# A planner that orders a kernel's instructions gets other numbers for its transfers: first landing later, 400 in place of 360

## The chip, the cores and the metric

The kernel runs on one core of a Trainium2 chip. The metric is device time in microseconds (us) of one execution, the median of several. Five engines take part: PE (TensorE, matrix products), DVE (VectorE), ACT (ScalarE), POOL (GpSimd) and SP (SyncE, which here only issues transfers). Each engine takes its instructions in the order in which they were emitted, and waits where an operand is not there yet.

## The reference, cut to what matters

```python
# x: (8, 8, 512, 64), state: (8, 8, 32, 64); weights are float64
a = softmax(scale * x @ state.T)         # per batch and head
xread = a @ state
a2 = softmax(scale * state @ x.T)
sread = a2 @ x
x = concat([xread, sread], tokens)       # 8 * 544 = 4352 tokens of 512
h = x @ w_in                             # 512 -> 1024
solu = h * softmax(h)
ln = layernorm(solu) * g_ln
y = ln @ w_out                           # 1024 -> 512
g = maximum(y @ w2_in, 0) ** 2           # 512 -> 2048
out = g @ w2_out                         # 2048 -> 512
```

## The kernel before, in words

Phase 1 goes batch by batch (b = 0 to 7). Per batch the kernel loads x in two layouts (xT and xn) and the block-diagonal states (bdf), makes the two score matrices (lines 358 to 470: products on PE, exponentials a_sb and eT on ACT at L433 and L400, sums, reciprocals and the scaling at L443 on DVE and POOL), builds the products sw of the state and the first layer's weights, and runs the first layer (hps, L635), the SoLU and the layer norm (L593 to L624), the transposes of its result (lnTp, L687; split in lt at L693 on ACT and L696 on DVE) and the second layer (y, L722). Most products are made in three passes over operands that are split in a high and a low part (a cast at L262 on ACT gives the high one, a subtraction at L268 on DVE or POOL the low one). Where PE turns to a piece that is not there, it waits.

The weights come as float64 and are decoded on the chip (`decode`, L284 to L327): a transfer of 512 KB into a buffer `raw` (three of them; `raw_u` at the start), an activation on ACT at L312 that reads it into `wi`, `dec` or `w`, a shift at L315 and a combination at L318 on DVE, and for most of them the cast and the subtraction. w_in and w_out are decoded at the start, into wi and wo. Later in phase 1 the weights of the third and fourth layers are decoded beside the other work, four pieces of 512 KB at a time, in six stretches, whose first loads are issued at about 108, 157, 206, 250, 295 and 339 us (the rest of the fourth layer's from 387 us on). They are summed as Strassen's method wants them, split in `w2s` and stored in DRAM as `w_d`.

Phase 2, from about 421 us on, makes the last two layers by Strassen's method, seven products instead of eight (h at L1144 and L1289 are its products on PE). It reads y back from DRAM (`yraw`), makes its sums (`load_y`, L891 to L941: yt, casts on ACT and subtractions and sums on DVE), and reads the weights from `w_d` into `w`.

The order of PE's work is written out by hand, in the order in which the program calls. The order of the other engines is not. All their work is given as tasks to a planner, the class `Flow` (line 31 on). It keeps one clock per engine in `free`, for DVE (V), ACT (A), POOL (P) and the transfers (D), and steps its own time `now` forward with PE's written order. `poll` goes through the tasks by how soon their results are due and emits the next instruction of a task once the task's operands are planned to be there and the engine planned to be free. `run` gives the planned end, which is the operand's time for the task's next step. So the planned time of a transfer decides which instructions stand in front of the one that reads what it brings, in each engine's queue. The kernel is planned twice, and the second plan uses the due times that the first one found. A transfer goes through `dma`, and its cost is its size over a rate:

```python
def run(self, eng, cost, ready, emit):
    start = max(self.free[eng], ready, self.now)
    self.free[eng] = start + cost
    emit(eng)
    return start + cost + (2.0 if eng == "D" else self.HOP)
...
def dma(out, in_, kb):
    return fl.run("D", kb / 360.0, 0.0, lambda e: nc.sync.dma_start(out=out, in_=in_))
```

All transfers are issued from SP in the order in which the planner emits them. Names: `wi`, `wo`, `dec`, `w` decoded weights; `w2s` and `w_d` split weights and their place in DRAM; `sps`, `hps`, `sTp`, `aTp`, `lnTp`, `ep`, `xsp`, `y`, `h` tiles in PSUM that PE writes; `ys` a copy of y that is stored; `u`, `e` the SoLU's tiles.

Of the kernel before, what the change touches and what calls it, by code (L numbers as in the profile page):

```python
# [31 lines left out]
class Flow:  # L32
# [12 lines left out]

    SPARE = {"V": 0.7, "A": 0.0, "P": 0.0, "D": 0.0}
    NEVER = 1e9

    def __init__(self, plan=None):

        self.plan, self.made = plan, []
        self.now = 0.0
        self.end = 0.0
        self.warm = self.WARM_UP
        self.free = {"V": 0.0, "A": 0.0, "P": 0.0, "D": 0.0}
        self.tasks = []
        self.later = []

# [9 lines left out]
    def spawn(self, gen, slack=8.0):  # L68


        task = {"gen": gen, "req": None, "done": None, "slack": slack, "costs": [],
                "by": self.NEVER, "n": len(self.made)}
        self.made.append(task)
# [36 lines left out]
    def latest(self, task):  # L110

        if self.plan:
            by, costs = self.plan[task["n"]]
            if by < self.NEVER:
                return by - sum(costs[len(task["costs"]):])
# [49 lines left out]
def attn_solu_relu2_kernel(  # L165
# [14 lines left out]
    nc = tc.nc  # L180
# [6 lines left out]
    B, P, T, _ = x_n.shape  # L187
    S = x_t.shape[3]
    HP = x_t.shape[2]
    H, D = 2 * HP, P // 2  # L190
# [13 lines left out]
    fl = Flow(plan)  # L204
# [36 lines left out]
    room = {"raw": 3, "dec": 3, "e": 2, "raw2": 3, "dec2": 2, "u": 8, "g": 3}  # L241

    def dma(out, in_, kb):
        return fl.run("D", kb / 360.0, 0.0, lambda e: nc.sync.dma_start(out=out, in_=in_))

    def take(name):
        def ok():
# [36 lines left out]
    def decode(dst_h, dst_l, src, pool=None, w=None, spare=False):  # L284
# [15 lines left out]
        if len(src.shape) == 3:  # L300
            tf = tf.rearrange("p (k f) -> p k f", k=src.shape[1])
        f = dma(tf, src, 512)
        own = w is None
        if own:
# [37 lines left out]
    def load_x(b):  # L342
        bdf[b] = ap_.tile([P, G, 192], F32, tag="bdf", name="bdf", bufs=2)
        done["st", b] = dma(bdf[b], bd[b], 192)
        xT[b] = ap_.tile([P, HP, S], F32, tag="xT", name="xT")
        done["xT", b] = dma(xT[b], x_t[b], 1024)
# [544 lines left out]
    def load_y(j):  # L891
        t0, n = groups[j]
        q = n * P
        for _, name, _ in PRODUCTS:
            done["y", j, name] = {"by": fl.NEVER, "done": None}

# [484 lines left out]
```

## Time and profile before

| | |
|---|---|
| median of 3 runs | 1096.95 us (1093.66 to 1098.14) |
| the profiled execution's own time | 1096.98 us |
| its span in the profile | 1095.1 us |
| mean granted clock of PE | 0.991 |
| PE busy | 1065.5 us, 97% of the span |
| DVE, ACT, POOL busy | 786.7, 589.4, 144.2 us |

The span lies 1.9 us below the execution's own time. PE is busy nearly throughout; the about 30 us in which it is not lie mostly ahead of 60 us. A row of the timeline gives the start in us from the span's start, the duration, the engine and line, the operation with output and input, and in brackets the idle time ahead of it on its engine with what ended it.

### The profile page before, as it was taken

How to read it: one execution, taken by the hardware profiler on the slowest of the kernel's cores; microseconds unless marked ns; L12 is line 12 of the kernel's file. 1: busy time of each engine (PE TensorE's matmuls, PEld its weight loads, DVE VectorE, ACT ScalarE, POOL GpSimd, SP SyncE). 2: the span in 40 equal slices, each digit the busy share in tenths (PEclk: the TensorE clock that was granted, in tenths of full speed). 3: DMA queues.
4: the chain of work that ended last, by engine and by line, in shares of the span. 5: the costliest groups of instructions: out<-in, count | busy, mean ns of one | idle time of the engine just before them, and what ended most of it. 6: DMA issues, size and time to landing. Idle time of an engine off the chain costs nothing.

```text
span 1095.1 us, 19407 instructions
## 1 busy us (share of the span) xinstructions
PE 1065.5 (97%) x7184; PEld 941.0 (86%) x7184; DVE 786.7 (72%) x1243; ACT 589.4 (54%) x992; POOL 144.2 (13%) x229
## 2 busy tenths in 40 slices
PE   4999998999999999999999999999999999999998
PEld 1467777777777888889998889999999999999998
DVE  6856776888887867868984479755688467855773
ACT  4948677787787765435453344533345334533442
POOL 1623332333434320000000000000000000000000
PEclk8989999999999999999999999999999999999999
DMA  9420553747526378998787777778889888898885
GB/s 352 169 85 24 177 211 124 278 146 244 212 87 241 138 259 272 309 320 260 193 249 229 195 201 204 231 233 265 253 270 304 282 252 277 264 312 254 249 262 159
DMA packets 126509, 247.70 MB, mean 226 GB/s; under 512 B 13520, under 2 KB 36048, under 8 KB 124368
## 3 DMA queue, kind: packets, MB, share of 16 engines
q1 hardware_dynamic: 126416, 246.47, 69.5%
q8 instruction: 57, 0.93, 0.4%
q14 instruction: 36, 0.29, 0.1%
HBM read 199.23 MB, written 47.19 MB: 225 GB/s over the span
## 4 chain that ended last, share of the span: by engine, by line
PE 89%; ACT 4%; DVE 3%; DMA 2%; issue 1%; POOL 1%; SPq 0%; ACTq 0%; DVEq 0%; POOLq 0%
PE h L1289 31%; PE h L1144 30%; PE y L722 15%; PE hps L635 7%; PE lnTp L687 2%; PE hps L376 1%; DMA raw_u<-w_in 1%; ACT u L624 1%; PE aTp L470 1%; DMA raw<-w_in 1%; ACT e L603 1%; PE srd L486 1%; PE sTp L414 0%; DMA raw<-w_out 0%; PE sps L376 0%
## 5 line engine op out<-in xcount | busy, mean ns | idle before, releaser
L1289 PE MATMUL h<-w,g 128*128 128x256 f32 x2856 | 343.5, 283 | 0.0
L1289 PEld LDWEIGHTS h<-w,g 128*128 128x128 f32 x2856 | 343.3, 192 | 0.2
L1144 PE MATMUL h<-yt,w 128*128 128x384 f32 (+1 forms) x1680 | 328.2, 356 | 0.5 <-ACT ys L262 0.5
L1144 PEld LDWEIGHTS h<-yt,w 128*128 128x128 f32 x1680 | 300.6, 188 | 27.0 <-ACT ys L262 0.7
L722 PE MATMUL y<-lt,wo 128*128 128x512 f32 (+1 forms) x864 | 219.2, 396 | 2.1 <-DVE sw L268 1.7
L262 ACT CAST g<-r 128x768 fp32r<-128x768 f32 (+1 forms) x140 | 128.3, 920 | 150.9 <-PE h L1289 147.6
L268 DVE TENSOR_TENSOR g<-r,g 128x768 fp32r<-128x768 f32 (+1 forms) x140 | 148.4, 1063 | 51.8 <-ACT g L262 51.2
L722 PEld LDWEIGHTS y<-lt,wo 128*128 128x128 f32 x864 | 150.3, 191 | 37.9 <-issue 6.7
L1108 DVE TENSOR_TENSOR r<-u,h 128x384 f32<-128x384 f32 (+1 forms) x120 | 72.1, 604 | 109.5 <-PE h L1144 109.1
L1094 ACT COPY u<-h 128x512 f32<-128x512 f32 (+2 forms) x160 | 81.3, 522 | 112.0 <-PE h L1144 85.4
L1190 DVE TENSOR_TENSOR r<-r 128x768 f32<-128x768 f32 (+1 forms) x100 | 104.9, 1060 | 21.1 <-ACT r L1180 20.8
L635 PE MATMUL hps<-sw,aT 128*128 128x512 f32 x368 | 98.3, 417 | 0.0
L635 PEld LDWEIGHTS hps<-sw,aT 128*128 128x128 f32 x368 | 69.8, 192 | 23.5 <-issue 6.2
L696 DVE SCALAR_TENSOR_TENSOR lt<-lnTp,g_sb,lt 128x512 fp32r<-128x512 f32 (+1 forms) x72 | 51.6, 716 | 25.6 <-ACT lt L693 24.8
L1182 DVE SCALAR_TENSOR_TENSOR r<-r 128x768 f32<-128x768 f32 (+3 forms) x80 | 65.2, 834 | 1.2
L1094 ACT ACTIVATE r<-h 128x384 f32<-128x384 f32 (+1 forms) x40 | 21.2, 531 | 82.3 <-PE h L1144 81.9
L693 ACT ACTIVATE lt<-lnTp,g_sb 128x512 fp32r<-128x512 f32 (+1 forms) x72 | 47.7, 662 | 31.4 <-PE lnTp L687 31.3
L268 POOL TENSOR_TENSOR w2s<-dec,w2s 128x512 fp32r<-128x512 f32 (+1 forms) x38 | 47.9, 1273 | 70.3 <-ACT w2s L262 50.3
L598 DVE SCALAR_TENSOR_TENSOR u<-u,e 128x1024 f32<-128x1024 f32 x34 | 42.5, 1249 | 5.9 <-ACT e L593 5.5
L268 DVE TENSOR_TENSOR yt<-yraw,yt 128x384 fp32r<-128x384 f32 (+1 forms) x70 | 41.3, 606 | 6.3 <-ACT yt L262 6.1
L687 PE MATMUL lnTp<-ident,u 128*128 128x128 f32 x272 | 42.6, 275 | 1.1 <-ACT u L624 1.1
L624 ACT ACTIVATE u<-u,nmu,vs 128x1024 f32<-128x1024 f32 x34 | 42.1, 1241 | 2.5 <-POOL nmu L619 2.5
(98 smaller groups left out, 909.6 us busy)
## 6 DMA issues: line engine op xcount, KB each, us to landing
w<-w_d SPq DMA_DIRECT2D x560, 256.0 KB, 3.4
w_d<-w2s SPq DMA_DIRECT2D x36, 512.0 KB, 3.2
raw<-w_out SPq DMA_DIRECT2D x24, 512.0 KB, 6.7
xT<-x_t SPq DMA_DIRECT2D x8, 1024.0 KB, 7.0
xn<-x_n SPq DMA_DIRECT2D x8, 1024.0 KB, 6.1
y_d<-ys SPq DMA_DIRECT2D x16, 512.0 KB, 3.7
raw<-w_in SPq DMA_DIRECT2D x16, 512.0 KB, 7.9
out<-u SPq DMA_DIRECT2D x28, 256.0 KB, 2.8
```

The source lines that it names most:

```text
L262: nc.scalar.copy(out=out, in_=in_)
L268: return lambda e: eng_of[e].tensor_tensor(out=out, in0=in0, in1=in1, op=ALU.subtract)
L624: f = yield {"A": 1.16}, f, lambda e: nc.scalar.activation(out=u, in_=u, func=AF.Identity, bias=nmu, scale=c)
L635: nc.tensor.matmul(out=ps, lhsT=lhsT(i, k), rhs=rhs(j, k)[:, cs], start=(k == 0 and n == 0), stop=(k == n_k - 1 and n == len(passes) - 1),)
L687: nc.tensor.transpose(ps[:, t, :], u_t[key, t][:, k * P:(k + 1) * P], ident)
L722: nc.tensor.matmul(out=ps, lhsT=wo[k][:, w, c * P:(c + 1) * P], rhs=o[:, a], start=(k == 0 and i == 0), stop=(k == K1 - 1 and i == 2),)
L1094: nc.scalar.activation(out=o, in_=src, func=func) if func else nc.scalar.copy(out=o, in_=src)
L1108: f = yield {"V": 0.15 + cols / 960}, max(at, box["task"]["done"]), lambda e: nc.vector.tensor_tensor(out=o, in0=box["t"], in1=src, op=ALU.add
L1144: nc.tensor.matmul(out=ps, lhsT=wt[:, e2, k], rhs=yy[:, e1, k], start=(p in ("P1", "P2", "P5") and k == 0 and s == 0), stop=(k == 1 and s ...
L1182: f = yield {"V": 0.15 + (2 - key[-1]) * q / 960}, f, lambda e: nc.vector.scalar_tensor_tensor(out=v, in0=v, scalar=0.0, in1=v, op0=ALU.ma ...
L1190: return lambda e: eng_of[e].tensor_tensor(out=out, in0=in0, in1=in1, op=op)
L1289: nc.tensor.matmul(out=where[i // 2][0][:, i % 2 * Q:i % 2 * Q + Q], lhsT=g[:, e1, m % 2, i * P:i * P + P], rhs=wt[:, e2], start=(p in ("P ...
```

## The change

The transfers' clock starts at 2.6 us instead of 0, and a transfer costs its KB over 400 instead of over 360. So a transfer of 512 KB is planned at 1.28 us instead of 1.42, and the first transfers land 2.6 us later in the plan, less what the rate gives back.

```diff
     SPARE = {"V": 0.7, "A": 0.0, "P": 0.0, "D": 0.0}
     NEVER = 1e9
+    FIRST_DMA = 2.6
...
-        self.free = {"V": 0.0, "A": 0.0, "P": 0.0, "D": 0.0}
+        self.free = {"V": 0.0, "A": 0.0, "P": 0.0, "D": self.FIRST_DMA}
...
     def dma(out, in_, kb):
-        return fl.run("D", kb / 360.0, 0.0, lambda e: nc.sync.dma_start(out=out, in_=in_))
+        return fl.run("D", kb / 400.0, 0.0, lambda e: nc.sync.dma_start(out=out, in_=in_))
```

No instruction is given other work. The order of PE's 6,722 instructions stays as it was; on DVE, ACT, POOL and SP instructions change places, and ten subtractions of the low parts go from POOL to DVE. All lines of the changed kernel lie one further down. Three places follow. (In these rows a count as x3 stands for instructions of the same kind in a row, and the numbers behind a name are those of its buffers.)

ACT at the start, from the decode of the fifth piece of w_in on (wi), with the two exponentials of the first softmax (a_sb), the copies sw and aT and the first pieces of w_out (dec); before:

```order
L312 ACTIVATE wi_126<-raw_u 128x512
L312 ACTIVATE wi_127<-raw_u 128x512
L433 ACTIVATE a_sb<-a_sb 128x512
L312 ACTIVATE wi_128<-raw_u 128x512
L262 COPY sw<-hps 128x512
L312 ACTIVATE wi_129<-raw_u 128x512
L262 COPY sw<-hps 128x512
L433 ACTIVATE a_sb<-a_sb 128x512
L262 COPY aT<-aTp 128x512
L312 ACTIVATE dec<-raw 128x512 x3
```

and now:

```order
L313 ACTIVATE wi_126<-raw_u 128x512
L313 ACTIVATE wi_127<-raw_u 128x512
L313 ACTIVATE wi_128<-raw_u 128x512
L434 ACTIVATE a_sb<-a_sb 128x512
L313 ACTIVATE wi_129<-raw_u 128x512
L263 COPY sw<-hps 128x512 x2
L313 ACTIVATE dec<-raw 128x512
L434 ACTIVATE a_sb<-a_sb 128x512
L263 COPY aT<-aTp 128x512
L313 ACTIVATE dec<-raw 128x512 x3
```

The first exponential has moved behind the seventh piece of w_in, the second one behind the first piece of w_out. Some rows on, four decodes instead of three stand ahead of the first SoLU's exponential (L593).

ACT in the second stretch with such decodes (about 155 to 177 us), from the copy xs on; dec are pieces of the third layer's weights, L693 the high part of lt, L593, L603 and L624 the SoLU and the layer norm; before:

```order
L262 COPY xs<-xsp 128x4x32
L693 ACTIVATE lt<-lnTp,g_sb 128x512
L593 ACTIVATE e,es<-u,hm 128x1024
L262 CAST w2s<-dec 128x2x256
L603 ACTIVATE e,vs<-u,us 128x1024
L312 ACTIVATE dec<-raw 128x512
L400 ACTIVATE eT,l_1705<-s_sb,m_1718 128x512
L433 ACTIVATE a_sb<-a_sb 128x512
```

and now:

```order
L263 COPY xs<-xsp 128x4x32
L263 CAST w2s<-dec 128x2x256
L694 ACTIVATE lt<-lnTp,g_sb 128x512
L594 ACTIVATE e,es<-u,hm 128x1024
L313 ACTIVATE dec<-raw 128x512
L604 ACTIVATE e,vs<-u,us 128x1024
L401 ACTIVATE eT,l_1712<-s_sb,m_1725 128x512
L434 ACTIVATE a_sb<-a_sb 128x512
```

The cast w2s has moved ahead of lt, and a first decode ahead of the SoLU's L603. Up to the last L603 and L693 of this stretch ACT now has four decodes where it had three. In the next three of these stretches (from 206, 250 and 295 us on) a decode likewise now stands ahead of the first L603, and four instead of three come within the stretch; the fourth came some 13 us or more later before.

ACT at the end of phase 1 (about 418 to 425 us), with the last copies of y (ys), the casts yt of the first products' operands and the decodes and casts of the fourth layer's weights (w); before:

```order
L262 CAST yt<-yraw 128x512
L262 COPY ys<-y_4438 128x256
L262 COPY ys<-y_4439 128x256
L262 CAST yt<-yraw 128x512
L262 COPY ys<-y_4440 128x256
L262 COPY ys<-y_4441 128x256
L312 ACTIVATE w_4282<-raw 128x512
L1094 COPY u_4642<-h_4629 128x512
```

and now:

```order
L263 COPY ys<-y_4443 128x256
L263 COPY ys<-y_4444 128x256
L263 COPY ys<-y_4445 128x256
L263 CAST yt<-yraw 128x512
L263 COPY ys<-y_4446 128x256
L263 CAST yt<-yraw 128x512
L263 CAST w_4283<-w_4283 128x256
L263 CAST w_4282<-w_4282 128x2x256
```

The casts yt have moved two places back, one of them in between the last two copies of y, and casts of weights stand where the first copies of h were. On SP a load of w_out, which needs a free raw buffer, has moved ahead of the twelve loads of `w` that were issued from 387.60 us on.

## Rows read from the trace of the kernel before

**Rows 1.** The page: busy time by engine.

```profile
PE 1065.5 (97%) x7184; PEld 941.0 (86%) x7184; DVE 786.7 (72%) x1243; ACT 589.4 (54%) x992; POOL 144.2 (13%) x229
```

**Rows 2.** Busy time by stretches; the last three columns: granted clock, DMA share, GB/s.

```profile
0.00:27.40 27.40, 11.06 (x64) 3.83 (x64) 16.67 (x35) 11.82 (x19) 3.03 (x8) 0.88 0.94 352
27.40:54.80 27.40, 24.70 (x188) 11.05 (x172) 24.39 (x49) 24.86 (x47) 17.14 (x25) 0.93 0.45 169
150.00:180.00 30.00, 26.71 (x210) 20.75 (x195) 19.94 (x43) 19.30 (x36) 7.64 (x15) 0.96 0.72 252
180.00:330.00 150.00, 150.00 (x1039) 115.73 (x1038) 127.75 (x247) 117.31 (x207) 56.45 (x91) 1.00 0.51 179
500.00:1095.10 595.10, 591.28 (x4181) 577.99 (x4179) 403.54 (x521) 249.61 (x395) 0.00 (x0) 1.00 0.80 245
```

**Rows 3.** PE's waits: for whom, us in total, times, longest.

```profile
PE aTp L470 <- POOL a_sb L443: 7.6, 2, 4.1
PE sTp L414 <- DVE lt L696: 3.3, 1, 3.3
PE h L1144 <- ACT ys L262: 0.5, 1, 0.5
```

**Rows 4.** Timeline of ACT, from the sixth piece of w_in to the first SoLU.

```profile
14.83 0.67 ACT L312 ACTIVATE wi<-raw_u 128x512 f32<-128x512 f32 x1 [0.61 <-DMA raw_u<-w_in]
16.11 0.67 ACT L312 ACTIVATE wi<-raw_u 128x512 f32<-128x512 f32 x1 [0.61 <-DMA raw_u<-w_in]
17.24 0.63 ACT L433 ACTIVATE a_sb<-a_sb 128x512 f32<-128x512 f32 x1 [0.46 <-DVE a_sb L268]
17.77 0.66 ACT L312 ACTIVATE wi<-raw_u 128x512 f32<-128x512 f32 x1
...
21.68 0.63 ACT L433 ACTIVATE a_sb<-a_sb 128x512 f32<-128x512 f32 x1 [1.74 <-DVE a_sb L268]
...
23.72 0.67 ACT L312 ACTIVATE dec<-raw 128x512 f32<-128x512 f32 x1 [0.38 <-DMA raw<-w_out]
```

**Rows 5.** Timeline of PE, around the second layer's start.

```profile
59.15 1.65 PE L722 MATMUL y<-lt,wo 128*128 128x512 f32 x3 [1.13 <-DVE sw L268]
```

**Rows 6.** Timeline of ACT in the second stretch with decodes.

```profile
174.38 0.66 ACT L312 ACTIVATE dec<-raw 128x512 f32<-128x512 f32 x1 [3.02 <-DMA raw<-w_in]
174.95 1.13 ACT L603 ACTIVATE e<-u,us 128x1024 f32<-128x1024 f32 x1
...
176.08 0.67 ACT L693 ACTIVATE lt<-lnTp,g_sb 128x512 fp32r<-128x512 f32 x1
```

**Rows 7.** Timeline of PE in the second stretch with decodes.

```profile
168.42 2.92 PE L635 MATMUL hps<-sw,aT 128*128 128x512 f32 x12
...
177.59 0.93 PE L414 MATMUL sTp<-ident,s_sb 128*128 128x128 f32 x4 [3.29 <-DVE lt L696]
179.59 3.71 PE L635 MATMUL hps<-sw,aT 128*128 128x512 f32 x12
```

**Rows 8.** Timeline of ACT in the third stretch with decodes.

```profile
219.79 1.15 ACT L603 ACTIVATE e<-u,us 128x1024 f32<-128x1024 f32 x1 [0.17 <-DVE u L598]
...
223.47 0.68 ACT L312 ACTIVATE dec<-raw 128x512 f32<-128x512 f32 x1 [1.69 <-DMA raw<-w_in]
```

**Rows 9.** Timeline of DVE in the third stretch with decodes.

```profile
221.96 0.75 DVE L696 SCALAR_TENSOR_TENSOR lt<-lnTp,g_sb,lt 128x512 fp32r<-128x512 f32 x1
```

**Rows 10.** Timeline of PE in the third stretch with decodes.

```profile
223.41 0.60 PE L414 MATMUL sTp<-ident,s_sb 128*128 128x128 f32 x4
```

**Rows 11.** Timeline of SP, at the end of phase 1: loads of w and of y.

```profile
387.60 9.67 SPq L244 DMA_DIRECT2D w<-w_d  x12
...
408.85 5.04 SPq L244 DMA_DIRECT2D yraw<-y_d  x2
```

**Rows 12.** Timeline of ACT, around the start of phase 2.

```profile
420.11 0.62 ACT L262 CAST yt<-yraw 128x512 fp32r<-128x512 f32 x1
420.63 0.65 ACT L262 COPY ys<-y 128x256 f32<-128x256 f32 x2
```

## The prediction

> **What bounds the kernel now.** I read the page first: PE is busy 97% of the span [rows 1]. The order of PE's instructions does not change, and neither does any instruction's work, so the time can only move where PE waits, or begins to wait, and where its clock falls behind a wait. The table by stretches says where that is [rows 2]: of the 29.6 us in which PE is not busy, 16.3 lie in the first 27.4 us and 2.7 in the next 27.4; 3.3 lie at 150 to 180 us; there is nothing at 180 to 330 us, and 3.8 after 500 us, where no wait on another engine is listed, so that is start and tail of a dense stretch. The list of PE's waits names the causes [rows 3]: the scaled softmax a_sb of the first batch (7.6 us in two waits), one wait of 3.3 us in the second stretch with decodes, and the copy ys at the start of phase 2 (0.5); about 60 us there is one of 1.13 for sw [rows 5]. Behind that PE is dense but for these, so what is lost or gained at the start is carried to the end.
>
> Next I asked which of the planner's numbers is right, since that is what the change is about. At the start ACT waits for each piece of w_in, and the decodes begin at 14.83 and 16.11 us, each at the end of such a wait [rows 4]: 1.28 us for 512 KB, which is 400 KB per us, not 360. So the new rate is the truer one for that stretch. That says the plan comes nearer to the transfers, not that the kernel gets shorter: an engine that takes its work in order loses wherever the plan puts a decode ahead of work that PE waits for and the piece lands later than planned.
>
> The Trainium skill speaks against the change here: its page "DMA: Bandwidth & Descriptors", section "Specifications", gives a limit of about 358 GB/s for the memory of one core, by which a piece of 512 KB (524 kB) takes 1.46 us and the old rate would have been the right one. The measured 1.28 us is 410 GB/s, so this trace does not show that limit at the start.
>
> **The start: +1.4 us.** ACT's first exponential of a_sb began at 17.24 us, ahead of the seventh piece of w_in, and was followed by it 0.53 us later [rows 4]. Now the seventh piece stands ahead. It lands one piece's spacing after the sixth, at 16.11 + 1.28 = 17.39 us, so the exponential begins at 17.39 + 0.53 = 17.92, 0.68 us later. The second exponential began at 21.68; now the first piece of w_out stands ahead of it. The second piece had landed at 23.72, the end of a wait [rows 4], so the first one landed at about 23.72 - 1.28 = 22.44, and the exponential begins at 22.44 + 0.53 = 22.97, 1.29 us later. Both lead by way of DVE and POOL to the aTp for which PE waits [rows 3]. Some of this is taken back where DVE's sums had their own work ahead of them; I take 1.0, about the middle. Then a fourth decode stands ahead of the first L593, at 0.53 us. From there to 54.8 us ACT is busy 24.86 and DVE 24.39 of 27.4 us [rows 2], so the two of them set the pace and hardly catch up; I let 0.4 of the 0.53 stand. PE meets it at 59.15 us, where it already waits 1.13 us for sw and three products then take 1.65 us [rows 5]. Sum +1.4. Bounds: 0 if the cover in front of 55 us is larger than it looks; above, 1.29 + 0.53 = 1.8 and 0.7 more of lower clock, +2.5.
>
> **The second stretch with decodes: +1.3 us.** PE waited 3.29 us for L696, which waits for the L693 at 176.08 on ACT [rows 6, 7]. That stood behind L603 (174.95), and this behind the third decode, which had waited 3.02 us for its piece (174.38) [rows 6]. Now a fourth decode stands there too. If the pieces are issued as before, the fourth lands one spacing later, at 174.38 + 1.28 = 175.66. L603 follows after 0.57 us and L693 after 1.13 more, as the rows' starts say, so L693 begins at 177.36 and not 176.08: +1.28, and PE is later by that. Behind the wait PE's clock was at the lower of its two levels for a while (mean 0.96 in the stretch [rows 2]); the same twelve products took 3.71 us behind it and 2.92 ahead of it [rows 7]. The cast w2s that moved ahead of the first L693 may wait for its buffer, but the lt behind it is used one round later on PE. Bounds: 0, if the earlier decodes free buffers earlier and the pieces come sooner; +2.5 with a longer time at the lower clock.
>
> **The next three such stretches: +1.2 us.** PE does not wait there now (150.00 busy of 150.00 [rows 2]). In the one at 206 us L603 began at 219.79, and the third decode came behind it, at 223.47, after a wait [rows 8]. Now both late decodes stand ahead. On SP a store less stands ahead of the second piece, so the pieces should come some 2 us sooner, and then L603 is late by one to two decodes, 0.6 to 1.2 us. PE's cover there is 0.7 us: the L696 on which its sTp waits ends at 222.71 [rows 9], and sTp begins at 223.41 without a wait [rows 10]. I take +0.4 for each of three. Bounds: 0 each, and 1.3 each, as in the second stretch; the case in which the pieces do not come sooner is a rival below.
>
> **The turn to phase 2: +0.8 us.** PE waited 0.5 us for the last copies of y [rows 3]. A cast of yt stood ahead of the last two and now stands between them; one place costs 420.63 - 420.11 = 0.52 us [rows 12]. The loads of w now go out behind a load that waits for a buffer, some 11 us later; they took 9.67 us from 387.60 on [rows 11], so they would be out at about 409, with 12 us of cover to 421. The second load of yraw comes later, with the casts that need it; 0.3 us for that. Bounds: 0, if the copies' wait has room; +4, if yraw's second load, which already held SP for most of 5.04 us [rows 11], is late for the sums by as much as that.
>
> **What costs nothing.** The orders after 430 us shift by a place or two. PE is dense there, and the loads of w run ahead of it. The ten subtractions moved from POOL to DVE lie where DVE has room; DVE is busy 127.75 of 150 us in its fullest stretch [rows 2]. If that cover went, each would cost up to 0.7 us of DVE.
>
> **Sum.** 1.4 + 1.3 + 1.2 + 0.8 = +4.7 us on the profiled execution's 1096.98, 1101.7 us. That execution is the median of the runs to 0.03 us, so the forecast for the median is the same. The bounds add up to 0 and +12.9, 1097 to 1110 us.
>
> **Rivals.**
>
> *Faster: the wait at 177 us goes.* The truer plan may put L603 ahead of the pieces that are late, or bring the pieces sooner. Then the 3.29 us go, and with them the slow products: 3.71 - 2.92 = 0.79 us for those twelve [rows 7], and, as an estimate, 1 us for the fewer ones around them. With the start unchanged that is -5.1 us, 1091.9 us; with something won at the start too, 1090. For it: the rate is right now. Against it: a further decode stands in front of exactly that L693. Chance 0.18, of which 0.11 lies beyond 0.5%, since it needs little more than the 5.1 us.
>
> *Slower: the wait comes in the stretches at 206 and 250 us as well.* One mechanism: both late decodes stand ahead of L603, and their pieces land when they did. Then the fourth lands at 223.47 + 1.28 = 224.75, L693 comes 0.57 + 1.13 us later, at 226.45, where by the same steps from 219.79 it came at about 221; less 0.7 us of cover PE waits 4.7 us, and with 1.8 of lower clock behind it 6.5. The stretch at 250 us is much alike, I put it at 5.8; the one at 295 us has its pieces early. With 1.4, 1.3 and 0.8 from above it makes +15.8, 1112.8 us. It decides itself at whether the third piece lands before about 221 us. For it: the waits for pieces in rows 6 and 8. Against it: the store less on SP. Chance 0.17. By the rule of the skill's page on a memory limit of 358 GB/s it would be the likelier, since every piece would land later than the new plan has it; the 1.28 us speak against it.
>
> *Nothing: the order changes and PE does not notice.* All moves stay within the cover, 1097 us. For it: PE has the same order and waits little. Against it: two of the moves stand in front of things that PE waits for already. That the change does little is in here. Chance 0.20.
>
> **How the numbers follow.** A measurement of this kernel can tell about 0.5%, 5.5 us, from no change. My case (+2 to +10 us, likeliest +4.7) has 0.45, of which 0.25 lies within 0.5% and 0.20 beyond. So: faster 0.11; the same 0.07 + 0.20 + 0.25 = 0.52; slower 0.20 + 0.17 = 0.37. The range reaches from 1092, which leaves out half of the faster case, to 1112, which leaves out half of the slower one, 0.17 to 0.18 together.
>
> **What would show it.** In the profile of the changed kernel, step by step: PE's waits for a_sb 1 to 2 us longer in sum, and the second exponential at about 23 us; the one wait at about 178 us still there and over 4 us; new waits of under 1 us on the same line near 224, 269 and 313 us; a wait of about 1 us on ys at 421 to 425 us. It is wrong if the wait at 177 us is gone, if waits of over 3 us stand in the stretches at 206 and 250 us, or if the first exponential of a_sb begins at 17.3 us as before.

## The result and the profile after

The changed kernel took 1109.94 us in the median of five runs (1109.48 to 1112.24), before 1096.95 (five runs, 1093.66 to 1098.14): a ratio of 1.0137, with a 95% interval of 1.0120 to 1.0153. It is slower by 13 us where 4.7 were forecast. The range of 1092 to 1112 us holds the time. The profiled execution took 1109.94 us, its span is 1108.2 us.

The page's first line: PE was busy as long as before, to 0.1 us [rows 1].

```profile
PE 1065.5 (96%) x7184; PEld 937.7 (85%) x7184; DVE 786.1 (71%) x1252; ACT 590.6 (53%) x993; POOL 133.4 (12%) x219
```

So in sum the 13.1 us of span are time in which PE is not busy. The equal sums hide two differences, which show when the same instructions are followed in both timelines: up to 183 us on the clock of the kernel before, PE's instructions are busy 154.6 us instead of 158.5, since its clock is higher about 60 us and behind 177 us, and those behind 183 us are busy 911.1 us instead of 907.1, since the clock is lower behind some of the new waits. The waits of PE by cause, over the whole span, to hold against [rows 3]:

```profile
PE aTp L471 <- POOL a_sb L444: 8.0, 3, 4.6
...
PE sTp L415 <- DVE lt L697: 6.2, 4, 2.2
PE hps L636 <- DVE s_sb L388: 2.5, 2, 2.4
...
PE y L723 <- ACT lt L694: 2.2, 2, 1.5
...
PE y L723 <- DVE lt L697: 1.8, 2, 1.6
...
PE h L1145 <- ACT ys L263: 0.8, 1, 0.8
```

The one wait on lt ahead of sTp has become four, of 6.2 us in sum, and two lines of waits of y on lt are new. The table of stretches gives the places. Of the kernel before, the stretches that did not stand among [rows 2]:

```profile
54.80:82.10 27.30, 24.84 (x177) 18.80 (x177) 15.04 (x35) 13.59 (x26) 6.91 (x10) 0.87 0.24 85
...
370.00:421.00 51.00, 50.12 (x286) 43.15 (x284) 32.89 (x58) 29.97 (x56) 13.56 (x17) 1.00 0.74 262
421.00:500.00 79.00, 78.94 (x357) 65.61 (x358) 63.23 (x98) 37.72 (x69) 0.00 (x0) 1.00 0.89 301
```

and of the changed kernel:

```profile
0.00:27.40 27.40, 9.98 (x56) 3.93 (x64) 16.20 (x33) 11.90 (x19) 3.04 (x8) 0.89 0.95 352
...
54.80:82.10 27.30, 24.04 (x185) 17.35 (x186) 15.20 (x35) 14.83 (x29) 5.86 (x9) 1.00 0.24 85
...
150.00:180.00 30.00, 26.13 (x204) 20.23 (x197) 20.24 (x43) 18.97 (x36) 9.25 (x15) 1.00 0.73 252
180.00:330.00 150.00, 145.15 (x994) 111.37 (x993) 120.19 (x246) 113.08 (x198) 45.58 (x82) 0.99 0.48 175
...
370.00:421.00 51.00, 47.20 (x237) 38.56 (x236) 33.95 (x59) 32.60 (x58) 13.65 (x19) 1.00 0.63 227
421.00:500.00 79.00, 77.17 (x371) 64.00 (x372) 63.62 (x100) 38.39 (x72) 0.00 (x0) 1.00 0.88 302
```

PE was busy without a gap at 180 to 330 us and now loses 4.85 us there; at 370 to 500 us it loses 5.6 where it lost 0.9. The start loses more busy time than before as well, but that is not the end of it, as the next reading shows. PE's order is the same in both kernels, so the same instruction can be looked up in both timelines, and the difference of its starts is how far PE lags:

| PE instruction | start before | start after | lag, us |
|---|---|---|---|
| sTp, second batch | 48.08 | 50.62 | 2.5 |
| ep | 53.35 | 56.10 | 2.8 |
| y, first group | 56.91 | 58.36 | 1.5 |
| lnTp | 64.86 | 64.82 | 0.0 |
| lnTp, end of the second stretch with decodes | 183.14 | 182.08 | -1.1 |
| sTp, third stretch | 223.41 | 223.88 | 0.5 |
| lnTp, fourth stretch | 271.50 | 275.85 | 4.4 |
| sTp, fifth stretch | 311.77 | 317.69 | 5.9 |
| y | 368.64 | 375.44 | 6.8 |
| y, last tokens of phase 1 | 410.79 | 420.35 | 9.6 |
| h, start of phase 2 | 421.06 | 432.69 | 11.6 |
| h, fourth layer | 1030.65 | 1043.03 | 12.4 |

This is the table from which all else follows: nothing from the start, about 7 us from the three stretches that begin at 206, 250 and 295 us, nearly 6 us from there to the start of phase 2, most of it at the turn, 0.8 early in phase 2, and the last 0.7 of the span behind the table's end. ACT in the fourth stretch (the one at 250 us before) shows the mechanism:

```profile
265.71 0.67 ACT L313 ACTIVATE dec<-raw 128x512 f32<-128x512 f32 x1 [1.11 <-DMA raw<-w_in]
...
267.11 0.67 ACT L313 ACTIVATE dec<-raw 128x512 f32<-128x512 f32 x1 [0.21 <-DMA raw<-w_in]
267.68 1.14 ACT L604 ACTIVATE e<-u,us 128x1024 f32<-128x1024 f32 x1
268.81 0.67 ACT L694 ACTIVATE lt<-lnTp,g_sb 128x512 fp32r<-128x512 f32 x1
```

and PE behind it:

```profile
270.31 0.75 PE L415 MATMUL sTp<-ident,s_sb 128*128 128x128 f32 x4 [2.16 <-DVE lt L697]
...
272.15 3.86 PE L636 MATMUL hps<-sw,aT 128*128 128x512 f32 x12
```

The third and the fourth decode each wait for their piece, L604 stands behind both, lt behind L604, PE waits 2.16 us for lt, and the twelve products that follow take 3.86 us. PE's mean granted clock from 270 to 276 us is 0.72. In the kernel before, the same L603 and the same twelve products, at a granted clock of 1.00:

```profile
264.00 1.15 ACT L603 ACTIVATE e<-u,us 128x1024 f32<-128x1024 f32 x1 [0.35 <-DVE u L598]
```

```profile
268.75 2.91 PE L635 MATMUL hps<-sw,aT 128*128 128x512 f32 x12
```

In this stretch the lag grows by 3.9 us.

### The profile page after: what moved, and what is told of

It reads as the page before. It is cut to its first block, busy times and chain, and to the rows that moved or that the text cites. A ratio compares the mean times of both kernels' runs of the same rounds, so it can differ in the third digit from the quotient of the medians.

```text
span 1108.2 us, 19399 instructions
## 1 busy us (share of the span) xinstructions
PE 1065.5 (96%) x7184; PEld 937.7 (85%) x7184; DVE 786.1 (71%) x1252; ACT 590.6 (53%) x993; POOL 133.4 (12%) x219
## 4 chain that ended last, share of the span: by engine, by line
PE 76%; DMA 10%; ACT 5%; DVE 4%; issue 3%; POOL 1%; SPq 0%; ACTq 0%; POOLq 0%; DVEq 0%
PE h L1290 31%; PE h L1145 29%; PE y L723 8%; PE hps L636 4%; DMA raw<-w_out 4%; DMA raw<-w_in 3%; DMA w_d<-w2s 2%; PE lnTp L688 1%; DMA w<-w_d 1%; PE hps L377 1%; ACT u L625 1%; ACT e L604 1%; POOL w2s L269 1%; DMA raw_u<-w_in 1%; ACT dec L313 1%
## 5 line engine op out<-in xcount | busy, mean ns | idle before, releaser
L269 POOL TENSOR_TENSOR w2s<-dec,w2s 128x512 fp32r<-128x512 f32 (+1 forms) x29 | 35.7, 1235 | 73.1 <-ACT w2s L263 73.1
```

Of the source, the lines that this page charges most:

```text
L269: return lambda e: eng_of[e].tensor_tensor(out=out, in0=in0, in1=in1, op=ALU.subtract)
```

## The experiments

**Which of the two numbers.** With the later start alone (2.6 us, rate 360) the planner writes the very order of the kernel before, on every engine; with the rate alone (no later start, rate 400) that of the change. So the later start does nothing, and all that follows is about the rate.

**Where it costs.** Three runs put the new rate into one part of the plan alone. The first, only while PE's planned time is under 150 us:

```diff
-        return fl.run("D", kb / 400.0, 0.0, lambda e: nc.sync.dma_start(out=out, in_=in_))
+        return fl.run("D", kb / (400.0 if fl.end < 150 else 360.0), 0.0, lambda e: nc.sync.dma_start(out=out, in_=in_))
```

> Both constants of the change, but the new rate of 400 only while PE's planned time is under 150 us; from there on 360. Theory A (what the trace of the change shows): the start costs nothing by the end, since PE's lag behind the kernel before rises to 2.75 us at 56 us and is back at 0 by 65 us; so 0, within -1.5 and +1.5 us of before. Rival B (the start's later exponentials are carried to the end, as predicted): +1.4 us or more; rival C (any other order than the one tuned for 360 costs time): slower by some us here too.

Measured: 1094.99 us against 1095.51, a ratio of 0.9998 (0.9987 to 1.0009). The start costs nothing, though PE's lag in this profile too rises to 2.85 us at 53 us. The second, up to 340 us (`fl.end < 340`):

> The same with the new rate up to 340 us of planned time, 360 behind it: start and the stretches with decodes alone. Theory A: the lag that the trace of the change has gained by 340 us, -1.0 at 183, +1.5 at 223, +3.8 at 267 to 276, +1.6 at 302 to 318, in all about +6 us over before (5 to 7), with PE's new waits on L696 at 224, 270 and 317 us. Theory D (the loss lies in the turn to phase 2 alone, and what is late at 340 us is caught up there): 0 to +1.

Measured: 1103.20 us, 1.0073 (1.0053 to 1.0093), +8 us, a little more than expected. PE's lag is 0 at 183 us, 5.4 at 271, 6.6 at 312 and 8.0 at 369 us, and the four waits on L696 sum up to 5.0 us. The third, from 340 us on:

```diff
-        return fl.run("D", kb / 360.0, 0.0, lambda e: nc.sync.dma_start(out=out, in_=in_))
+        return fl.run("D", kb / (360.0 if fl.end < 340 else 400.0), 0.0, lambda e: nc.sync.dma_start(out=out, in_=in_))
```

> 360 up to 340 us of planned time, 400 behind it: the turn to phase 2 alone. Theory A: the lag gained after 340 us in the trace of the change, 0.9 at 368, 4.8 at 408 to 432 and 0.75 at 497 us: about +6.4 us over before (5.5 to 7.5), SP held by the second load of a piece of w_out for over 8 us in front of the twelve loads of w. Theory D: +12 or so. If neither place costs anything alone (the two only cost together), 0.

Measured: 1102.51 us, 1.0063 (1.0043 to 1.0083), +7 us, as expected. So the two places cost 8 and 7 us, each by itself; that is 15 us together, about the 13 that the change costs.

**Why in the stretches with decodes.** If the decodes cost because the plan has their pieces land too soon, then a plan that has them land later must cure it, whatever the rate. The whole change, with 4 us more for a piece:

```diff
-        f = dma(tf, src, 512)
+        f = dma(tf, src, 512) + (4.0 if fl.end > 100 else 0.0)
```

> The whole change, and the plan takes each 512 KB piece of float64 weights to land 4 us later than it did, once PE's planned time is over 100 us (the traces show 5 to 9 us from issue to landing there, the plan 3.3). The decodes then stand behind L603 and behind most of L433 in the stretches from 157 us on. Theory A (decodes stand ahead of their pieces): the waits on L696 at 224, 270 and 317 us go, the time falls by 5 us or more below the change, to at most +5 us over before, and to that of before or lower if the turn is cured with it. Rival C (any order other than the one tuned for 360 costs): as slow as the change, +10 us or more.

Measured: 1095.34 us, 0.9998 (0.9988 to 1.0007). The 13 us are gone, at the rate of 400, in an order that differs from that of before in hundreds of rows. The waits of sTp on L696 are gone, and PE's longest wait between 150 and 380 us is 0.73 us. Rival C falls with it. And the other way round: the kernel before, at 360, with 2 us less for a piece (`- (2.0 if fl.end > 100 else 0.0)`):

> The kernel before, rate 360 and no later start, but the plan takes each 512 KB piece of float64 weights to land 2 us earlier than it did, once PE's planned time is over 100 us. Four decodes then stand ahead of the last L603 in the stretches from 157 us on, and the second load of w_out ahead of the loads of w, as in the change. Theory A (the planned landing of these pieces is all that matters): +8 us or more over before, with waits on L696 near 224, 270 and 317 us. Rival F (the rate matters by what it does to the stores and the other loads, of 128 to 1024 KB): within 3 us of before.

Measured: 1113.25 us, 1.0170 (1.0147 to 1.0194), +17 us, more than the change. PE's waits from 100 to 520 us, first line:

```profile
PE sTp L414 <- DVE lt L696: 8.6, 4, 3.7
```

These four waits stand at 183, 230, 276 and 323 us. So pieces that are planned to land too early are enough for a loss of this size, at the old rate too, and pieces planned later undo it, at the new rate too. That the rate costs by nothing else is not shown, and the last run below speaks against it. 400 has a piece land 0.14 us sooner than 360 (512/360 - 512/400), and sooner still where other transfers are queued ahead of it; these two were not run apart. How far off the plan is in either case, the trace of the kernel before shows. The median time from issue to landing, of the pieces issued from 100 us on, which are those of the third layer's weights (w_in in these rows) and of the fourth's (w_out):

```profile
raw<-w_in SPq DMA_DIRECT2D x16, 512.0 KB, 7.9
raw<-w_out SPq DMA_DIRECT2D x16, 512.0 KB, 5.8
```

The plan has 1.28 + 2.0 = 3.28 us or, at 360, 3.42, when nothing is queued ahead of the piece on the planned clock. The Trainium skill's page "DMA: Bandwidth & Descriptors", section "Anatomy of one DMA — SWDGE (gpsimd) path", has a fit of about 2.0 us plus the bytes over 436 GB/s; as an estimate by it, a piece of 512 KB would take 3.2 us. That is near what the plan has, and it is said there of the gpsimd path, each transfer for itself; in this kernel, on SP's queue and among stores and other loads, the trace shows 5.8 and 7.9 us, about twice that.

**Why at the turn.** SP in the changed kernel, loads of w_out (raw), of w and stores of y:

```profile
391.69 14.10 SPq L245 DMA_DIRECT2D raw<-w_out  x2
405.88 7.06 SPq L245 DMA_DIRECT2D w<-w_d  x12
413.35 0.33 SPq L245 DMA_DIRECT2D raw<-w_out  x1
```

ACT and PE in the changed kernel:

```profile
419.27 0.66 ACT L313 ACTIVATE w<-raw 128x512 f32<-128x512 f32 x1 [2.53 <-DMA raw<-w_out]
419.84 0.46 ACT L694 ACTIVATE lt<-lnTp,g_sb 128x256 fp32r<-128x256 f32 x1
```

```profile
420.35 1.98 PE L723 MATMUL y<-lt,wo 128*128 128x256 f32 x12 [1.51 <-ACT lt L694]
```

The second load of w_out waits on SP for a free buffer, 14.1 us together with the first. Before it, SP had the twelve loads of w out by 397 us [rows 11]. Now they go out from 405.88 on, and the next load of w_out behind them, at 413.35. Its decode stands on ACT in front of lt, waits for it until 419.27, and PE waits 1.51 us for lt. (The two lines of waits of y on lt in the list above have 4.0 us in sum.) To see whether this place in SP's queue is the cause, the run with the rate from 340 us on was given one condition more, in `prepared`, which puts the second and later of these loads behind the twelve:

```diff
+    n_all = []
     def source(kind, m, h):
...
+            if kind[1] > "2" and h + m > EARLY_W3: yield None, 0.0, lambda: len(units) <= n_all[0] - WR
             f = yield from decode(None, None, source(kind, m, h), w=w[h])
...
-    units.reverse()
+    units.reverse(); n_all.append(len(units))
```

> As the run with 400 from 340 us on (+7 us over before), with one thing undone: the second and later pieces of the last w_out weights are not loaded before the twelve loads of w have been issued, as the order before had it by itself. Theory A (the second load of w_out stands on SP in front of the twelve loads of w and of all that follows, waits there for its buffer, and its decodes then make ACT late with lt): at most +2 us over before. Rival E (it is the late casts yt between the copies of y, or the casts of the weights between them, that cost): still +5 us or more.

Measured: 1095.87 us, 1.0001 (0.9990 to 1.0013): all of the 7 us are gone. SP in this run:

```profile
381.27 0.63 SPq L244 DMA_DIRECT2D raw<-w_out  x1
382.00 9.60 SPq L244 DMA_DIRECT2D w<-w_d  x12
394.54 0.33 SPq L244 DMA_DIRECT2D raw<-w_out  x1
```

In this order the casts yt too stand again where they stood before, so the run by itself does not part Theory A from rival E. The waits do: behind 380 us, PE in the run with 400 from 340 us on waits 4.4 us for lt and 0.9 for ys, which were 0.3 and 0.5 in the kernel before. So the casts between the copies of y can have cost about 0.4 of the 7 us.

**How late is late enough.** The wait at 177 us of the kernel before [rows 7] is of the same kind. So later pieces ought to make it faster. First 4 us between 100 and 340 us of planned time, with the change up to 340 us and the rate of 360 behind it, and then with the kernel before:

```diff
-        f = dma(tf, src, 512)
+        f = dma(tf, src, 512) + (4.0 if 100 < fl.end < 340 else 0.0)
```

> The change up to 340 us of planned time with the pieces taken to land 4 us later between 100 and 340 us, and 360 without that behind 340 us. Theory A: the gain that the run with late pieces had at 183 us (-4.5 us, the wait of 3.3 us at 177 us and its slow products gone) is kept and the turn is that of before: -3 to -4.5 us against before. If it is given back at the turn whatever stands there: within 1.5 us of before.

> The kernel before, rate 360, with the pieces taken to land 4 us later between 100 and 340 us of planned time, nothing else. Theory A: the same as with the rate of 400, -3 to -4.5 us against before. If the rate has a gain of its own there, no more than -1.

Measured: 1096.22 us, 1.0008 (0.9999 to 1.0018), and 1094.85 us, 0.9990 (0.9981 to 0.9999). Theory A failed in both; the first lies where it was said to lie if the gain is given back, the second between its two cases. The profiles of the two are 4.6 and 5.5 us ahead of that of before at 183 us and then give back 1.8 us by 385 us and 2.7 by 369 us, presumably because decodes that come later press on what follows; that was not tried. Such a lead of one profile over another is a weak measure, though: the run with w ahead of w_out has the order of before up to 340 us, and its profile too is 4.3 us ahead at 183 us, with a wait of 2.05 us in place of 3.29 and a higher clock. So the medians decide. Then 2 and 6 us, with the kernel before:

> The kernel before, rate 360, pieces taken to land 2 us later between 100 and 340 us of planned time (the run before this one had 4 us there and gained 0.1%). Theory A: the plan only has to be late enough that no decode stands ahead of its piece; 2 us puts two decodes back behind L433 and L693, so within 2 us of before, and no wait over 2 us on L696. If every allowance below the measured 5 to 9 us costs, +3 us or more.

> The same with 6 us. Theory A: no wait for pieces left, but the decodes and the casts w2s that follow them come later and bunch up ahead of the turn; so within 2 us of before, most of the gain at 177 us given back by 385 us. If later is always better: -2 us or more.

Measured with 2 us: 1091.39 us against 1095.56, 0.9964 (0.9952 to 0.9976), faster than both kernels, where at most 2 us either way had been expected. With 6 us: 1105.88 us, 1.0096 (1.0075 to 1.0116), where 2 us at most had been expected too. With 2 us, ACT in the second stretch:

```profile
168.89 1.14 ACT L603 ACTIVATE e<-u,us 128x1024 f32<-128x1024 f32 x1
...
171.09 0.69 ACT L693 ACTIVATE lt<-lnTp,g_sb 128x512 fp32r<-128x512 f32 x1 [0.45 <-PE lnTp L687]
172.55 0.69 ACT L312 ACTIVATE dec<-raw 128x512 f32<-128x512 f32 x1 [0.77 <-DMA raw<-w_in]
```

No decode stands ahead of that L603 and L693 any more; PE is 5.8 us ahead of the profile of before at 183 us and still 5.8 at 1031 (4.2 by the medians), since from 70 to 520 us it waits 0.5 us in all. With 6 us, ACT and SP at the turn:

```profile
395.34 0.68 ACT L693 ACTIVATE lt<-lnTp,g_sb 128x512 fp32r<-128x512 f32 x1
403.42 1.14 ACT L262 CAST yt<-yraw 128x512 fp32r<-128x512 f32 x2 [7.41 <-DMA yraw<-y_d]
```

```profile
391.93 5.22 SPq L244 DMA_DIRECT2D w_d<-w2s  x4
397.21 2.00 SPq L244 DMA_DIRECT2D yraw<-y_d  x2
```

Here nothing is lost up to 397 us on the clock of the kernel before (PE is 6.0 us ahead), and then 16 us by 405 us: the last pieces' stores stand on SP in front of the loads of yraw, the cast of yt stands on ACT in front of lt and waits 7.41 us for them, and PE waits 10.8 us on lt. It looks like the same kind of error at another place; when the plan had these stores and that load was not looked up. The last run was the change up to 340 us with 2 us:

> The change up to 340 us of planned time with the pieces taken to land 2 us later between 100 and 340 us, 360 behind it. Theory A: the piece is then planned 3.28 + 2 us after its issue, later than the plan before had it (3.42), so the +8 us of the run with 400 up to 340 us are gone: within 2 us of before. If the rate of 400 costs there by itself: +4 us or more.

Measured: 1098.15 us, 1.0021 (1.0010 to 1.0032), +2.6 us, between the two that were expected: most of the 8 us are gone, but not as at 360, where the same 2 us made a kernel that is 6.8 us faster than this one. So at 400 something costs beyond the piece's own landing, which is planned later here than in the kernel before. PE waits 4.2 us for s_sb ahead of hps between 160 and 270 us; what makes the order differ from that at 360 with 2 us was not followed up.

## Why the prediction was wrong, point by point

**What bounds the kernel.** Right: the time moved where PE waits, and where its clock is lower behind a wait; PE's busy time is the same only because it is 3.9 us less up to 183 us and 4.0 more behind. That a piece takes 1.28 us at the start held as well (the changed kernel's ACT waits end at the same spacing), and that a truer rate need not help was the right warning.

**The start, +1.4 us.** Wrong, measured 0. The steps up to 56 us were right:

```profile
17.08 0.66 ACT L313 ACTIVATE wi<-raw_u 128x512 f32<-128x512 f32 x1 [0.61 <-DMA raw_u<-w_in]
17.64 0.62 ACT L434 ACTIVATE a_sb<-a_sb 128x512 f32<-128x512 f32 x1
...
22.13 0.67 ACT L313 ACTIVATE dec<-raw 128x512 f32<-128x512 f32 x1 [2.17 <-DMA raw<-w_out]
22.70 0.61 ACT L434 ACTIVATE a_sb<-a_sb 128x512 f32<-128x512 f32 x1
```

The exponentials begin at 17.64 and 22.70, forecast at 17.92 and 22.97, and PE lags by up to 2.8 us. The step that failed is that ACT and DVE "hardly catch up" and the lag is carried to the end. PE waited in the kernel before between 53 and 60 us anyway, and from 56 to 65 us the lag goes: 0.7 us of it in waits that are shorter, 2.1 because PE's products are faster. Six products of y took, in the kernel before,

```profile
61.30 2.91 PE L722 MATMUL y<-lt,wo 128*128 128x512 f32 x6
```

and in the changed one

```profile
61.94 2.02 PE L723 MATMUL y<-lt,wo 128*128 128x512 f32 x6
```

with a granted clock of 0.87 and 1.00 in the stretch of 54.80 to 82.10 us. That the clock would give this back no step of the prediction had, and what raised it stays open. The run with the new rate up to 150 us shows that the start costs nothing.

**The second stretch with decodes, +1.3 us.** Wrong in the size and the sign, measured -1.1 in the profiles. The fourth decode does stand ahead of L603, but its piece lands sooner than taken: it begins at 174.92 and not at 175.66. PE's wait moved, to 2.37 us in front of hps at 165.59 and 1.50 in front of sTp at 178.13, and the clock did not fall behind them. The -1.1 is no gain: the run with w ahead of w_out has the order of before up to 340 us, and its PE is 2.4 us further ahead at 183 us than behind 65 us when held against the profile of before. So executions of one order differ there by more than this.

**The next three, +1.2 us.** This is one of the two steps that failed. The mechanism was seen, both late decodes ahead of L603; the size was taken too small by a factor of six: the lag grows from -1.1 to 5.9 us, 7 us in three stretches. "L603 is late by one to two decodes, 0.6 to 1.2 us" counted only the decodes' own time and held that the pieces come sooner. They did, but not soon enough: in the fourth stretch L604 begins at 267.68 and was at 264.00 before, 3.2 us later than the lag of 0.5 explains. This stretch then pays twice, by the wait of 2.16 us and by the clock behind it. In the third and the fifth the clock stays at 1.00 behind waits of 1.47 and 1.05 us, and the lag grows by 1.5 and 1.6 us, which is still about four times the 0.4 that was taken. The slower rival had this mechanism, with 5.8 to 6.5 us for a stretch, and with two stretches. It came in three, with 1.5, 3.9 and 1.6 us, although the third piece of the stretch at 206 us was decoded from 218.91 us on, ahead of the rival's 221. That its 1112.8 us lies near the 1109.94 is luck: its price for a stretch was too high, its 2.7 us for the start and the second stretch did not come, and its turn was too low.

**The turn to phase 2, +0.8 us.** The other step that failed: about 5 us there in the profile of the change, 7 in the run with the turn alone, beyond the bound of 4. The wait for ys rose by 0.3 us, near the 0.5 that was costed for it. The loads of w were costed with 12 us of cover, and that held; what was not counted is what else stands behind the blocked load on SP, which is the next loads of w_out, and that their decodes stand on ACT in front of lt.

**The other rivals.** The wait at 177 us did not go with the change (1.50 us at 178 us and 2.37 at 166 us stand in its place), but in the runs with later pieces it is gone or down to 0.6 us, and so are its slow products. In the one with 2 us that was worth 4.2 us by the medians, where the rival had 5.1. That nothing would be noticed was right for the start alone.

**What costs nothing.** Right in what it named: no wait of PE lies behind 505 us; the subtractions on DVE are not seen in a wait.

## What to carry to other kernels

Where a planner sets the order of engines that work strictly in turn, a landing that is planned too early blocks an engine, and behind it work that the bottleneck waits for; one that is planned too late moves work into what follows. So take the time from issue to landing from the trace, among the other transfers, rather than the rate of one stream, and then vary it by some us in both directions; here, at the rate of 360, -2, 0, +2, +4 and +6 us gave +17, 0, -4, -1 and +10 us (the first to the end of the kernel, the others up to 340 us). The best of them, about 5.4 us from issue to landing, lies just under the measured medians of 5.8 and 7.9 us and not at them. When a transfer moves ahead in a queue, count everything that stands behind it there, up to the reader of the last of them.

## What the runs showed of the hardware

The 512 KB pieces come every 1.28 us at the start, in the changed kernel as before (410 GB/s). That rate does not tell when one lands: in the kernel before, the median from issue to landing was 10.3 us for the eight pieces of the first layer's weights at the start and 11.4 for the second's, and from 100 us on, between stores and loads of other kinds, 7.9 us for the third layer's and 5.8 for the fourth's.

PE's mean granted clock between 54.8 and 65 us went mostly, not always, with the order of the start: with the order of before it was 0.67 in six profiles and 0.83 in one, with that of the change 1.00 in five and 0.83 in one, though PE idles longer in the profile of the change than in that of before (3.26 and 2.46 us of the 10.2). Why was not tried.
